# Five transposes per quad instead of six, norm sums on GpSimd, and a reordered step in a two-layer recurrent kernel

## The chip, the cores and the metric

The kernel runs on one core of a Trainium2 chip. The metric is device time in microseconds for one execution of the whole program. Engines are called by their profile names: PE (TensorE) for matmuls and transposes, DVE (VectorE), ACT (ScalarE), POOL (GpSimd), and SP (SyncE), whose queue issues the weight DMAs.

## The reference

Four residual layers are applied to x of 2048 rows by 640: memory attention A, local attention B, then A and B again with the same weights.

```python
def A(x, mem):                       # 32 heads of 192; 64 segments of 32 rows, one after another
    for s in range(64):
        h = concat([mem, x[32*s:32*s+32]])          # 8 memory rows + 32 rows
        q, k, v = h@Wq, h@Wk, h@Wv                  # 640 -> 32 heads x 192
        p = softmax(where(mask, q@k.T * 192**-0.5, -1e9))
        o = (p @ v) @ Wo
        mem = o[:8];  out.append(o[8:])             # the next segment needs this memory
def B(x):                            # 32 heads of 20; each row sees rows s, s-2, ..., s-14
    q, k, v = split(x @ wqkv)
    return (softmax over the 8 rows of q.k * 20**-0.5) @ v @ wo
x = x + A(layernorm(x)); x = x + B(layernorm(x))
x = x + A(layernorm(x)); x = x + B(layernorm(x))
```

## The kernel before

The two passes through A and B are run side by side as two lanes. In step t, lane 0 does segment t of the first A layer and lane 1 does segment t-2 of the second; the B layers of step t-1 run in the same step. There are 67 steps: two with lane 0 alone, 62 with both lanes, two with lane 1 alone, and a last one with only the B layer of the last segment, whose order is the short list LAST. A full step handles 80 columns in layer A (two lanes of 8 memory and 32 data rows) and 64 in layer B. Activations are kept transposed, features on the partitions.

The 32 heads of A are handled as eight quads. A quad has 768 features, six chunks of 128: heads of 192 features share a chunk in pairs, and chunks 1 and 4 are the shared ones. Per quad and step:

- K, Q, V: 30 matmuls each of 128x128 weights against 80 columns (L303). KE and VE copy the result to SBUF on ACT (L329, L342), QE on DVE.
- S: scores (L368). E: exponential on ACT (L374). EM: mask on DVE (L380).
- T: PE transposes V, chunk by chunk (L349), and TE copies the transposed chunks on DVE into Vt (L357, L358).
- PO: probabilities times V and the row sums (L401), from Vt. R: one over the row sums on ACT (L388 twice, L390). OT1, OT2: the product on DVE (L408, L413, L414).
- Oa, Ob: the two halves of the output matmuls (L420), which add into two PSUM buffers held for the whole step. Quad 7's are O7x, O7y, O7z.

V and its transpose before the change:

```python
vt = self.VT[:, 0:6 * NT].rearrange("p (a n) -> p a n", a=6)
self.nc.scalar.copy(out=vt[:, :, self.cs], in_=...six chunks of 80 columns...)
for n in range(6):
    nc.tensor.transpose(out=ps[:, n, :], in_=self.VT[:, NT * n:NT * n + P], identity=self.ident[:])
```

At the end of a step MEMa and MEMb (L454) cast the new memory rows into hT, the input of the next step's projections, and X1 (L510) adds the residual. The layer norm of the next A input is LSQ (squares and sums over chunks, L460 to L466), lst (a ones matmul that sums over partitions, L473), LMV (mean and variance on DVE), LR (two ACT operations, L490 and L492) and LAP (L500, L502). The B layer's norm is bsq, bst, bmv, br, bap with the same functions; then bq, bk, bv are the projections with bqE, bkE, bvE behind them, bs0 and bs1 the scores of each lane, be and eb their exponentials and masks, bt and btE the transpose of the values, bp, on, bo, boE, by, byE the rest. Both sums over chunks, of x and of its square, are DVE reductions:

```python
for j, v in enumerate((x, sq)):
    nc.vector.tensor_reduce(out=s[:, j, :], in_=v[:].rearrange("p c n -> p n c"), op=ALU.add, axis=mybir.AxisListType.X)
```

The order of everything is the hand-written list ORDER. Every engine executes its own instructions of the list strictly in that order, and waits where data or a buffer is missing. PSUM has four general buffers that are given out in turn to the K, Q, V, T, S, statistics and B results (the function `big`), one pair of banks for PO and two for the output sums. POOL has one instruction in a step, a copy that takes the next segment's rows (L655), at the head of the step.

The A weights are 128 pieces of 224 or 256 KB. N_RES = 79 of them stay in SBUF after their first load; the others are streamed in every step through a ring of eight buffers by SP's queue (L279), which waits until PE is done with the buffer. `resident_pieces` spreads the streamed ones evenly over the step by the positions in ORDER.

Of the kernel before, what the change touches and what calls it, by code (L numbers as in the profile page):

```python
# [38 lines left out]
N_RES = 79  # L39
PIECE = (8, 7)  # L40
O_ROWS = ((0, 2, 3), (5, 1, 4))

# [5 lines left out]
K0 Q0 bsq K0y QE0 KE0 V0 bst bmv VE0 Q1 S0 K1 T0 QE1 br bap E0 TE0 KE1 V1 S1 EM0 Q3 PO0 VE1 QE3 E1 bq T1 R0 K2  # L48
KE2 bqE TE1 Q2 K3 V2 QE2 OT10 S2 KE3 bk EM1 OT20 S3 PO1 VE2 E2 bkE Q4 T2 EM2 bs1 E3 QE4 V3 R1 K4 TE2 be1 VE3
Q5 OT11 OT21 KE4 PO2 R2 EM3 T3 eb1 bs0 be0 V4 QE5 Oa0 VE4 bv TE3 OT12 OT22 bvE Q6 S4 PO3 eb0 E4 bt R3 QE6 btE  # L50
K5 T4 EM4 K6 KE5 TE4 bp0 V5 OT13 Ob0 OT23 KE6 on0 S5 bp1 VE5 PO4 T5 Oa1 E5 R4 on1 TE5 V6 bo Q7 EM5 OT14 S6 boE
OT24 VE6 Ob1 E6 QE7 PO5 T6 EM6 TE6 by byE R5 K7 KE7 V7 S7 VE7 OT15 E7 OT25 LSQ PO6 EM7 Oa2 R6 T7 Ob2 Oa3 TE7
Ob3 OT16 OT26 Oa5 PO7 Oa6 R7 lst LMV Ob5 Oa4 Ob6 OT17 LR OT27 Ob4 LAP O7x O7y MEMa O7z MEMb X1
# [4 lines left out]
bsq bst bmv br bap bq bqE bk bkE bs0 be0 bv bs1 be1 eb0 bvE bt eb1 btE bp0 on0 bp1 on1 bo boE by byE  # L58
""".split()

def half_order():

    order = []
    for n in ORDER:
        if n[0] in "KQV" and len(n) == 2:
            order += [(n[0].lower(), int(n[1]), 0), (n[0].lower(), int(n[1]), 1)]
        elif n[:2] in ("Oa", "Ob"):
            order.append(("o", int(n[2]), int(n[1] == "b")))
        elif n == "O7x":
            order += [("o", 7, 0), ("o", 7, 1)]  # L70
    assert len(set(order)) == len(order) == 8 * NQUAD
    return order

def half_blocks(kind, i, h):

    if kind == "o":
        if i == NQUAD - 1:
            blocks = [(m, c) for c in range(NC) for m in O_ROWS[0] + O_ROWS[1]]
        else:
            blocks = [(m, c) for rows in O_ROWS for m in rows for c in range(NC)]  # L80
    elif (kind, i) == ("k", 0):
# [8 lines left out]
def resident_pieces():  # L90

    at, t = {}, 0.0
    for n in ORDER:
# [21 lines left out]
class Kernel:  # L115
    def __init__(self, ctx, tc, xT, m0T, wA, wqkv, wo, out):
# [22 lines left out]
        self.n_big = 0  # L139
        self.xt, self.ots, self.qxs, self.kp, self.qp, self.vp, self.tp = {}, {}, {}, {}, {}, {}, {}  # L140
# [3 lines left out]
    def build_consts(self):  # L144
# [33 lines left out]
        self.VT = pers("VT", [P, 6 * NT + 48], 1)[0]  # L178
# [112 lines left out]
    def span_of(self, t):  # L291
# [3 lines left out]
        self.cs = slice(LT * self.l0, LT * self.l1)  # L295

    def proj(self, ps, kind, i, h, t, chained=False):
# [3 lines left out]
        for k, (c, n) in enumerate(half_blocks(kind, i, h)):  # L301
            yield k
            self.nc.tensor.matmul(ps[:, NT * n + c0:NT * n + c1], lhsT=self.block(kind, i, h, k), rhs=hT[:, NT * c + c0:NT * c + c1],  # L303
# [36 lines left out]
    def vE(self, i):  # L340
        vt = self.VT[:, 0:6 * NT].rearrange("p (a n) -> p a n", a=6)
        self.nc.scalar.copy(out=vt[:, :, self.cs], in_=self.vp[i][:, 0:6 * NT].rearrange("p (a n) -> p a n", a=6)[:, :, self.cs])  # L342

    def a_t(self, i):

        nc = self.nc
        ps = self.big("ps_vt", (P, 6, P), BF16)
        for n in range(6):
            nc.tensor.transpose(out=ps[:, n, :], in_=self.VT[:, NT * n:NT * n + P], identity=self.ident[:])  # L349
        self.tp[i] = ps  # L350

    def tE(self, i):

        nc = self.nc
        ps, vt = self.tp[i], self.Vt[0:NT].rearrange("p (a j e) -> p a j e", a=2, e=P)
        src = ps[0:NT].rearrange("p (a j) e -> p a j e", a=2)
        nc.vector.tensor_copy(out=vt[:, :, 0:4:3, :], in_=src[:, :, 0:3:2, :])  # L357
        nc.vector.tensor_copy(out=vt[:, :, 1:3, 0:64], in_=src[:, :, 1, :].rearrange("p a (j e) -> p a j e", j=2))  # L358
# [75 lines left out]

    def acc_lanes(self, g):
# [20 lines left out]
    def ln_sq(self, x):  # L456
# [3 lines left out]
        nc.vector.tensor_tensor(out=sq[:], in0=x[:], in1=x[:], op=ALU.mult)  # L460
        s = self.bp.tile([P, 2, NX], F32, name="ln_s", tag="xc")
        for j, v in enumerate((x, sq)):
            nc.vector.tensor_reduce(out=s[:, j, :], in_=v[:].rearrange("p c n -> p n c"), op=ALU.add, axis=mybir.AxisListType.X)
        hl = sq[:].rearrange("p c n -> p (c n)")[:, 0:4 * NX].rearrange("p (j a n) -> p j a n", j=2, a=2)
        nc.vector.tensor_copy(out=hl[:, 0], in_=s[:])
        nc.vector.tensor_tensor(out=hl[:, 1], in0=s[:], in1=hl[:, 0], op=ALU.subtract)  # L466
        return hl

    def ln_stats(self, hl):
        nc = self.nc  # L470
        ps = self.big("ps_st")
        for j in range(2):
            nc.tensor.matmul(ps[:, 0:2 * NX], lhsT=self.ones[:], rhs=hl[:, j].rearrange("p a n -> p (a n)"), start=(j == 0), stop=(j == 1))  # L473
        return ps

    def ln_mv(self, ps):

        nc = self.nc
        m = self.bp.tile([P, NX], F32, name="ln_m")
        nc.vector.tensor_scalar(out=m[:], in0=ps[:, 0:NX], scalar1=1.0 / D, scalar2=None, op0=ALU.mult)  # L480
        v = self.bp.tile([P, NX], F32, name="ln_v")
        nc.vector.tensor_tensor(out=v[:], in0=m[:], in1=m[:], op=ALU.mult)
        nc.vector.scalar_tensor_tensor(out=v[:], in0=ps[:, NX:2 * NX], scalar=1.0 / D, in1=v[:], op0=ALU.mult, op1=ALU.subtract)
        return m, v

    def ln_r(self, mv):
# [366 lines left out]
```

The softmax here doesn't subtract the row's maximum and nothing guards it: scores larger than these inputs give would overflow.

## Time and profile before

| | |
|---|---|
| median of 3 runs | 3138.72 us (3137.41 to 3142.72) |
| profiled execution | 3140.52 us, span 3138.8 us |
| a step with both lanes | 46.6 us |
| last step, B layer alone | some 21 us |
| granted PE clock | 0.983 |

Three more lines of the page: the granted clock and the DMA share in 40 slices of the span, and the weight stream's issues. The clock is at full speed after the first 100 us and until the tail. The DMA engines are busy for eight tenths or more throughout, and a streamed piece lands 3.9 to 4.0 us after its issue.

```profile
PEclk6899999999999999999999999999999999999998
DMA  9988888888888888888888888888888888888885
...
w_ring<-in_wA_dram SPq DMA_DIRECT2D x1716, 256.0 KB, 3.9
```

### The profile page before, as it was taken

How to read it: one execution, taken by the hardware profiler on the slowest of the kernel's cores; microseconds unless marked ns; L12 is line 12 of the kernel's file. 1: busy time of each engine (PE TensorE's matmuls, PEld its weight loads, DVE VectorE, ACT ScalarE, POOL GpSimd, SP SyncE). 2: the span in 40 equal slices, each digit the busy share in tenths (PEclk: the TensorE clock that was granted, in tenths of full speed). 3: DMA queues.
4: the chain of work that ended last, by engine and by line, in shares of the span. 5: the costliest groups of instructions: out<-in, count | busy, mean ns of one | idle time of the engine just before them, and what ended most of it. 6: DMA issues, size and time to landing. Idle time of an engine off the chain costs nothing.

```text
span 3138.8 us, 185804 instructions
## 1 busy us (share of the span) xinstructions
PE 3063.2 (98%) x83160; PEld 3036.4 (97%) x83160; DVE 2358.2 (75%) x6883; ACT 1747.2 (56%) x3829; POOL 48.2 (2%) x162
## 2 busy tenths in 40 slices
PE   6899999999999999999999999999999999999996
PEld 5799999999999999999999999999999999999996
DVE  3577777777777777777777777777777777777775
ACT  2355556555556556556555655555655655655653
POOL 2000000000000000000000000000000000000000
PEclk6899999999999999999999999999999999999998
DMA  9988888888888888888888888888888888888885
GB/s 360 320 263 267 263 262 265 264 264 265 266 268 263 268 266 263 268 266 263 268 266 261 267 263 267 261 265 268 263 267 266 264 267 267 263 269 266 262 274 184
DMA packets 487807, 838.02 MB, mean 267 GB/s; under 512 B 54240, under 2 KB 261984, under 8 KB 487008
## 3 DMA queue, kind: packets, MB, share of 16 engines
q1 hardware_dynamic: 477648, 820.89, 83.2%
q8 instruction: 651, 10.67, 1.4%
q10 hardware_dynamic: 9360, 5.26, 0.6%
q14 instruction: 148, 1.21, 0.1%
HBM read 823.31 MB, written 2.62 MB: 263 GB/s over the span
## 4 chain that ended last, share of the span: by engine, by line
PE 95%; DMA 3%; issue 1%; DVE 1%; ACT 0%; SPq 0%; DVEq 0%; ACTq 0%
PE ps_k L303 18%; PE ps_q L303 18%; PE ps_v L303 18%; PE ps_vt L349 6%; PE ps_o L401 5%; PE ps_s L368 5%; PE ps_by L634 2%; PE ps_bq L523 2%; PE ps_bv L548 2%; PE ps_bk L523 2%; DMA w_ring<-in_wA_dram 1%; PE ps_bs L575 1%; PE ps_bo L598 1%; PE ps_bvt L561 1%; PE ps_st L473 0%
## 5 line engine op out<-in xcount | busy, mean ns | idle before, releaser
L303 PEld LDWEIGHTS <-w_ring 128*128 128x128 bf16 x17754 | 784.4, 100 | 19.4 <-DMA w_ring<-in_wA_dram 10.5
L388 ACT ACTIVATE R<-ps_o 64x320 f32<-64x320 f32 (+1 forms) x1056 | 448.5, 425 | 273.8 <-PE ps_o L401 223.6
L342 ACT CAST VT_140<-ps_v 128x480 bf16<-128x480 f32 (+1 forms) x528 | 288.9, 547 | 230.7 <-PE ps_v L303 227.6
L329 ACT CAST KF_121<-ps_k 128x480 bf16<-128x480 f32 (+1 forms) x264 | 144.1, 546 | 391.2 <-PE ps_k L303 383.3
L374 ACT ACTIVATE Em<-ps_s 80x320 bf16<-80x320 f32 (+1 forms) x528 | 223.3, 423 | 157.2 <-PE ps_s L368 110.7
L420 PEld LDWEIGHTS <-w_ring 128*128 128x128 bf16 x6600 | 291.2, 100 | 3.5 <-DMA w_ring<-in_wA_dram 2.6
L335 DVE CAST QT_127<-ps_q 128x320 bf16<-128x320 f32 (+1 forms) x264 | 127.1, 481 | 203.4 <-PE ps_q L303 203.4
L357 DVE COPY Vt_134<-ps_vt 80x512 bf16<-80x512 bf16 x528 | 219.2, 415 | 71.5 <-PE ps_vt L349 69.3
L349 PE MATMUL ps_vt<-ident,VT_140 128*128 128x128 bf16 x3168 | 267.7, 221 | 0.0
L408 DVE TENSOR_TENSOR OT<-ps_o,R 128x320 bf16<-128x320 f32 (+1 forms) x528 | 249.9, 473 | 22.3 <-ACT R L390 16.6
L329 ACT CAST KF_123<-ps_k 128x480 bf16<-128x480 f32 (+1 forms) x264 | 144.1, 546 | 205.6 <-PE ps_k L303 203.9
L390 ACT ACTIVATE R<-R 128x320 f32<-128x320 f32 (+1 forms) x528 | 244.0, 462 | 16.6
L401 PE MATMUL ps_o<-Em,Vt_134 80*128 80x80 bf16 (+1 forms) x4224 | 238.0, 199 | 1.4 <-issue 1.3
L335 DVE CAST QT_125<-ps_q 128x320 bf16<-128x320 f32 (+1 forms) x264 | 126.5, 479 | 143.1 <-PE ps_q L303 71.9
L349 PEld LDWEIGHTS <-VT_140 128*128 128x128 bf16 x3168 | 191.5, 99 | 0.1
L303 PE MATMUL ps_q<-hT_92,w_ring 128*128 128x80 bf16 (+1 forms) x3234 | 185.8, 201 | 3.7 <-DMA w_ring<-in_wA_dram 2.6
L303 PE MATMUL ps_q<-hT_90,w_ring 128*128 128x80 bf16 (+1 forms) x3234 | 186.3, 201 | 2.2 <-DMA w_ring<-in_wA_dram 1.5
L401 PEld LDWEIGHTS <-Vt_134 80*128 80x128 bf16 x4224 | 181.6, 98 | 1.0 <-issue 0.7
L303 PE MATMUL ps_k<-hT_90,w_ring 128*128 128x80 bf16 (+1 forms) x3003 | 172.7, 201 | 1.4 <-DMA w_ring<-in_wA_dram 0.7
L303 PE MATMUL ps_k<-hT_92,w_ring 128*128 128x80 bf16 (+1 forms) x3003 | 171.8, 201 | 1.4 <-issue 1.4
L380 DVE TENSOR_TENSOR Em<-Em,maskA 80x320 bf16<-80x320 bf16 (+1 forms) x528 | 163.2, 309 | 12.5 <-ACT Em L374 8.4
L414 DVE TENSOR_TENSOR OT<-ps_o,R 64x160 bf16<-64x160 f32 (+1 forms) x528 | 165.1, 313 | 7.3
(3084 smaller groups left out, 8305.2 us busy)
## 6 DMA issues: line engine op xcount, KB each, us to landing
w_ring<-in_wA_dram SPq DMA_DIRECT2D x1716, 256.0 KB, 3.9
w_ring<-in_wA_dram SPq DMA_DIRECT2D x1518, 224.0 KB, 4.0
out_dram<-YT_94 ACTq DMA_DIRECT2D x32, 80.0 KB, 3.7
wqkv_sb<-in_wqkv_dram SPq DMA_DIRECT2D x3, 800.0 KB, 7.7
wo_sb<-in_wo_dram SPq DMA_DIRECT2D x1, 800.0 KB, 7.4
w_k_00_386<-in_wA_dram SPq DMA_DIRECT2D x1, 256.0 KB, 2.8
w_k_10_405<-in_wA_dram SPq DMA_DIRECT2D x1, 256.0 KB, 3.8
w_q_10_438<-in_wA_dram SPq DMA_DIRECT2D x1, 256.0 KB, 4.6
```

Of the source, the lines that this page charges most:

```text
L303: self.nc.tensor.matmul(ps[:, NT * n + c0:NT * n + c1], lhsT=self.block(kind, i, h, k), rhs=hT[:, NT * c + c0:NT * c + c1], start=(h == 0 ...
L329: self.nc.scalar.copy(out=kf[:, :, self.cs], in_=self.kp[i][:, 0:6 * NT].rearrange("p (a n) -> p a n", a=6)[:, :, self.cs])
L335: nc.vector.tensor_copy(out=qt[:, :, 0:4:3, cs], in_=pv[:, :, 0:3:2, cs])
L342: self.nc.scalar.copy(out=vt[:, :, self.cs], in_=self.vp[i][:, 0:6 * NT].rearrange("p (a n) -> p a n", a=6)[:, :, self.cs])
L349: nc.tensor.transpose(out=ps[:, n, :], in_=self.VT[:, NT * n:NT * n + P], identity=self.ident[:])
L357: nc.vector.tensor_copy(out=vt[:, :, 0:4:3, :], in_=src[:, :, 0:3:2, :])
L374: self.nc.scalar.activation(out=e[0:NT, :, cs], in_=self.sv[i][0:NT, :, cs], func=ACT.Exp, scale=float(DH) ** -0.5)
L388: self.nc.scalar.activation(out=r[rows, :, :, self.cs], in_=d, func=ACT.Ln)
L390: self.nc.scalar.activation(out=rf, in_=rf, func=ACT.Exp, scale=-1.0)
L401: nc.tensor.matmul(ov[:, pr, b, self.cs], lhsT=vt[0:NT, 512 * pr + P * b:512 * pr + P * (b + 1)], rhs=em[0:NT, 2 * pr + b // 2, self.cs], ...
L408: self.nc.vector.tensor_tensor(out=ot[:, :, 0:3:2, cs], in0=self.ov[:, :, 0:4:3, cs], in1=self.r[i][:, :, :, cs], op=ALU.mult)
L420: self.nc.tensor.matmul(self.acc[c // 3][:, o:o + self.cs.stop - self.cs.start], lhsT=self.block("o", i, h, k), rhs=ot[:, m, self.cs], sta ...
```

## The change

Four things are changed, and ORDER with them.

1. The V result's chunk 1 is put first in PSUM (V_AT). VE copies the other five chunks as before, and puts chunk 1, cut into column groups of 32, 32 and 16, into columns 96 to 127 of the first three. Five transposes then carry all six chunks: rows 0 to 79 of the result hold five chunks, rows 96 to 127 the three pieces of chunk 1. TE copies the five on DVE, and the new step TF copies the three pieces on ACT.
2. The sum over chunks of x, in both layer norms, becomes three additions on POOL. The sum of squares stays on DVE.
3. The second output half of quad 6 is sorted by output chunk and runs as O6x and O6y; the statistics of the next A norm (lst, LMV) stand before PO7.
4. In the last step the B layer's norm, masks and expansions handle only lane 1's 32 columns, and bs0, be0, eb0 are left out of LAST.

VT grows, and N_RES falls from 79 to 78.

```diff
-N_RES = 79
+N_RES = 78
+V_AT = (1, 0, 2, 3, 5, 4)
...
 ORDER = """
-K0 Q0 bsq K0y QE0 KE0 V0 bst bmv VE0 Q1 S0 K1 T0 QE1 br bap E0 TE0 KE1 V1 S1 EM0 Q3 PO0 VE1 QE3 E1 bq T1 R0 K2
...
-OT24 VE6 Ob1 E6 QE7 PO5 T6 EM6 TE6 by byE R5 K7 KE7 V7 S7 VE7 OT15 E7 OT25 LSQ PO6 EM7 Oa2 R6 T7 Ob2 Oa3 TE7
-Ob3 OT16 OT26 Oa5 PO7 Oa6 R7 lst LMV Ob5 Oa4 Ob6 OT17 LR OT27 Ob4 LAP O7x O7y MEMa O7z MEMb X1
+K0 bsq K0y KE0 Q0 V0 QE0 bst Q1 S0 bmv VE0 QE1 E0 T0 br K1 TE0 KE1 TF0 V1 Q2 VE1 EM0 S1 PO0 bap QE2 E1 V2 R0
...
+bp1 OT22 QE5 E4 PO3 on1 EM4 R3 V5 T4 VE5 TE4 K6 OT13 Q6 S5 TF4 OT23 bp0 PO4 KE6 Oa0 Ob0 E5 QE6 on0 T5 R4 S6
+TE5 EM5 OT14 E6 V6 TF5 OT24 Q7 QE7 VE6 bo Ob1 PO5 boE T6 by TE6 R5 K7 TF6 byE EM6 KE7 OT15 V7 OT25 VE7 S7 PO6
+Oa2 E7 LSQ T7 Ob2 R6 Oa3 EM7 lst TE7 OT16 Ob3 Oa4 TF7 OT26 LMV PO7 Oa6 Oa5 O6x R7 OT17 OT27 Ob4 Ob5 O6y LR LAP
+O7x O7y MEMa O7z MEMb X1
 LAST = """
-bsq bst bmv br bap bq bqE bk bkE bs0 be0 bv bs1 be1 eb0 bvE bt eb1 btE bp0 on0 bp1 on1 bo boE by byE
+bsq bst bmv br bap bk bkE bq bqE bv bs1 be1 bvE eb1 bt btE bp0 on0 bp1 on1 bo boE by byE
...
     def vE(self, i):
-        vt = self.VT[:, 0:6 * NT].rearrange("p (a n) -> p a n", a=6)
-        self.nc.scalar.copy(out=vt[:, :, self.cs], in_=self.vp[i][:, 0:6 * NT].rearrange("p (a n) -> p a n", a=6)[:, :, self.cs])
+        ps, cs, copy = self.vp[i], self.cs, self.nc.scalar.copy
+        copy(out=self.VT[:, :, cs], in_=ps[:, NT:6 * NT].rearrange("p (a n) -> p a n", a=NC)[:, :, cs])
+        if cs.stop - cs.start == NT:
+            copy(out=self.VT[:, 0:3, P - 32:P], in_=ps[:, 0:96].rearrange("p (a n) -> p a n", a=3))
...
     def a_t(self, i):
-        for n in range(6):
-            nc.tensor.transpose(out=ps[:, n, :], in_=self.VT[:, NT * n:NT * n + P], identity=self.ident[:])
+        for n in range(NC):
+            nc.tensor.transpose(out=ps[:, n, :], in_=self.VT[:, n, :], identity=self.ident[:])
...
+    def tF(self, i):
+        ps = self.tp[i]
+        two = lambda v: v.rearrange("p (j e) -> p j e", j=2)[:, :, 0:64]
+        for j in range(3):
+            n = min(NT - 32 * j, 32)
+            self.nc.scalar.copy(out=two(self.Vt[32 * j:32 * j + n, 128:384]), in_=ps[96:96 + n, j, :].rearrange("p (j e) -> p j e", j=2))
...
     def ln_sq(self, x):
-        nc.vector.tensor_tensor(out=sq[:], in0=x[:], in1=x[:], op=ALU.mult)
-        for j, v in enumerate((x, sq)):
-            nc.vector.tensor_reduce(out=s[:, j, :], in_=v[:].rearrange("p c n -> p n c"), op=ALU.add, axis=mybir.AxisListType.X)
+        add(s[:, 2:4, ns], x[:, 0:2, ns], x[:, 2:4, ns])
+        add(s[:, 2, ns], s[:, 2, ns], s[:, 3, ns])
+        add(s[:, 0, ns], s[:, 2, ns], x[:, 4, ns])
+        nc.vector.tensor_tensor(out=sq[:, :, ns], in0=x[:, :, ns], in1=x[:, :, ns], op=ALU.mult)
+        nc.vector.tensor_reduce(out=s[:, 1, ns], in_=sq[:, :, ns].rearrange("p c n -> p n c"), op=ALU.add, axis=mybir.AxisListType.X)
```

Here `add` is a `nc.gpsimd.tensor_tensor` and `ns` the rows in use (`b_rows`), all 64 except in the last step.

## The prediction

> **What bounds the kernel now.** I read the page's busy table first, then the list of TensorE's waits, then one step of the timeline.
>
> ```profile
> PE 3063.2 (98%) x83160; PEld 3036.4 (97%) x83160; DVE 2358.2 (75%) x6883; ACT 1747.2 (56%) x3829; POOL 48.2 (2%) x162
> ...
> L349 PE MATMUL ps_vt<-ident,VT_140 128*128 128x128 bf16 x3168 | 267.7, 221 | 0.0
> ```
>
> TensorE is busy nearly always, and its matmuls overlap, so the 221 ns of a transpose are latency, not its share of the time. The chain of waits lists six transposes as one piece of 0.34 us, 0.056 us each. From 160 to 3028 us the waits view gives TensorE under 5 us of waiting in all. But its matmul ends are modelled, so a gap shorter than the drain doesn't show there. The timeline of the end of a step shows one (columns: start, length, engine and line, operation, count):
>
> ```profile
> 1533.25 0.46 PE L401 MATMUL ps_o<-Em,Vt_134 80*128 80x80 bf16 x8
> ...
> 1537.17 0.42 PE L420 MATMUL ps_acc_51496<-OT,w_o_11_1962 128*128 128x80 bf16 x7
> 1537.61 0.45 PE L303 MATMUL ps_k<-hT_90,w_k_00_386 128*128 128x80 bf16 x8
> ```
> ```profile
> 1533.80 0.88 ACT L388 ACTIVATE R<-ps_o 64x320 f32<-64x320 f32 x2 [1.68 <-PE ps_o L401]
> 1534.71 0.47 ACT L390 ACTIVATE R<-R 128x320 f32<-128x320 f32 x1
> ```
> ```profile
> 1535.21 0.49 DVE L408 TENSOR_TENSOR OT<-ps_o,R 128x320 bf16<-128x320 f32 x1
> ...
> 1536.29 0.49 DVE L500 TENSOR_TENSOR ln_xc<-xin_86,ln_m 128x320 f32<-128x320 bf16 x1
> 1536.88 0.56 DVE L502 TENSOR_TENSOR hT_90<-ln_xc,ln_r 128x160 bf16<-128x160 f32 x2
> 1537.36 0.20 DVE L454 CAST hT_90<-ps_acc_51495 128x48 bf16<-128x48 f32 x1
> ```
>
> Projection matmuls start 0.0358 us apart (30 in 1.075). Seven from 1537.17 are issued by 1537.42, yet K0 of the next step starts at 1537.61: 0.19 us idle, in each of the steps that I looked at. What ends that gap is the memory cast at 1537.56, and behind it a chain without a hole: PO7, R7, OT17 and OT27, LAP, MEMa. So a step has two parts. From K0 to PO7 (1491.18 to 1533.25, 42.07 us) TensorE's own work decides. From PO7 to the next K0 (4.36 us) a ScalarE and VectorE chain decides, and TensorE work put there only fills it.
>
> **What the Trainium skill says.** "TensorE: Matmul & The Clock Gate", section "Back-to-back issue gap", gives N/2.4 + 2.5 ns for a warm matmul, 55.8 ns at 128 columns; the trace's 0.34/6 agrees. "ScalarE: Activation LUTs", section "What ACT_TABLE_LOAD costs", gives 186 ns + 0.833 ns per element and an overlap of 93 ns between neighbours. The trace is a little cheaper (480 elements 546 ns, 320 elements 425). "GPSIMD Engine Reference", section 3.1, gives a two-input add about 2.6 cycles an element at 1.2 GHz, 2.2 ns; the trace has such an add only at 10 elements, at 203 ns.
>
> **The change part by part.** A full step is one with both lanes, from the K0 at 138.04 to that at 3028.21: 62 of them, 46.62 us each.
>
> Transposes: eight quads lose one each, 8 x 0.0558 = 0.446 us of TensorE work per step, all before PO7.
>
> The first layer's statistics matmul (lst, 0.11 us) moves from behind PO7 to before it. Output halves: nine before PO7 and five behind it, in both orders. So the first part becomes 42.07 - 0.446 + 0.111 = 41.74 us. The second part is the same chain in the same order on ScalarE and VectorE, so 4.36 us; TensorE's work there falls by 0.11, and the gap before K0 grows from 0.19 to 0.30. Step: 46.10 against 46.43, **-0.335 us**, over 62 steps **-20.8 us**.
>
> ScalarE: the V copy of 480 elements (0.547) becomes 400 (0.486, between the rows at 320 and 480) and 96 (0.25, from the row of 240 at 0.36), and three copies of 128 elements (0.275 each by the same slope) are new: +1.0 us a quad, 8 us a step, from 57% to about 75% busy. I cost it at nothing, and T7 is the place to test that: 2.27 us of TensorE work (four output halves and lst) lie between T7 and PO7, the least of the eight. After PO6 ScalarE runs R6 (1.38) and TF7 (about 0.65, neighbours overlapping), ready 2.3 us after PO6; PO7 comes 3.09 us after it. Behind TF7 on ScalarE stands only R7, which waits for PO7 anyway. For T4, the next (2.6 us), the PSUM buffer is wanted again by bp0, behind TF4 in the order. If a TF came too late the PV matmuls and the whole TensorE queue would wait; bounds 0 to 0.4 us a step, I take 0.03.
>
> VectorE: the second transpose copy falls from 256 to 128 elements (0.277 to 0.21) and a 0.70 us reduction leaves each of two norms: some 2 us a step less, hidden behind TensorE and so worth nothing, except in the tail.
>
> GpSimd: three dependent adds per norm. This is the added wait that I fear. X1 ends 0.67 us after K0 starts; GpSimd's queue then has the copy of the next rows (0.41), done at 1.21. Only then come the adds, of 128, 64 and 64 elements. Estimate: 203 ns at 10 elements plus 2.2 ns for each further one gives 0.46, 0.32, 0.32, and 0.1 between them (the idle time in the row of the small adds): 1.3 us, done at 2.6. The VectorE cast and subtraction (0.26 and 0.29) wait for them, done at 3.2; behind them in VectorE's queue stand QE0, then bmv. TensorE reaches the second bst matmul at 0.86 + 0.215 + 1.075 + 1.075 + 0.056 = 3.28 us. So there is hardly any margin: every tenth above 1.4 us for the three adds stops TensorE by a tenth per step. Bounds: 1.0 us if an add costs like GpSimd's one-input operations (nothing lost), 1.8 if sharing with VectorE slows them (0.4 lost). I take 0.03 us a step. The same adds for LSQ run while VectorE still has byE, EM6 and OT15 ahead, and hide.
>
> One resident piece fewer: 50 streamed pieces a step for 49, 0.92 us apart for 0.95. SyncE's queue waits for ring buffers that TensorE frees; eight buffers give about 7.4 us against 3.9 to 4.0 to landing, so it hides: 0, bounds 0 to +2 us in all. I count +0.3 for the first steps, where the weights are still arriving and TensorE waits for them. Output chunks O6 in two parts: same matmuls and weights, inside the second part of the step, nothing. The single-lane steps at both ends keep their gaps: -0.5 together.
>
> Tail. After the last output chunk the local layer runs alone for some 21 us, a chain from X1 to the store. With one lane: one reduction and the sums (1.55 us of VectorE) become three small adds (about 0.95) and the cast and subtraction shrink, -0.75; the three LN operations, the two of ScalarE and the single h2T multiply -0.4; the key product goes first and QX halves, but the value product now stands before bs1, +0.2; two exponentials instead of four (this row is 2.41 us) -1.2.
>
> ```profile
> 3118.55 0.68 DVE L463 TENSOR_REDUCE ln_s<-x_369 128x64 f32<-128x320 bf16 x1
> ...
> 3124.36 1.49 DVE L539 TENSOR_TENSOR QX<-ps_bq,pair_mask 128x1280 bf16<-128x1280 f32 x1 [1.58 <-PE ps_bq L523]
> ```
> ```profile
> 3126.79 2.41 ACT L581 ACTIVATE EB_142<-ps_bs 64x512 bf16<-64x512 f32 x4 [4.61 <-PE ps_bs L575]
> ```
>
> Tail together -2.2 us (bounds -3.5 and 0).
>
> Sum: -20.8 + 62 x 0.06 (3.7 for the two waits) - 2.2 - 0.5 + 0.3 = -19.5. Against the profiled span of 3138.8 that is 3119.3. That execution took 3140.5 by the clock of the other runs, whose median is 3138.7, so spans stand level with the median within 0.1%. I forecast 3119 us.
>
> **The rivals.** *The chain does not bind.* If the 4.36 us shrink with the work (say the gap before K0 has another cause, such as the step's own first weights), the whole 0.446 us counts: -27.7 - 2.2 - 0.5, 3108.5 us. For it: the waits view names no such wait. Against: MEMa ends 0.05 us before K0 starts.
>
> *GpSimd's adds become the bound,* at bst, early in each step. Price: each step loses what the three adds take above 1.4 us. At 1.77 us the per-step gain is gone; at 2.0 us a step is 0.6 - 0.335 = 0.265 us longer, 16 us in all, less the tail: 3153 us, slower than before. It decides from about 1.9 us. For it: the margin is zero by my sum, and no row shows such adds at size. Against: the estimate is 1.3 us, and VectorE, from which a disturbance would come, has only a one-input reduction to do then.
>
> *ScalarE comes late,* 0.05 us on each of eight quads: 0.4 a step eats the gain, 3141 us. For it: 8 us more a step in a strict queue. Against: 0.8 us of margin at the tightest place.
>
> **How the numbers follow.** The forecast's case (3112 to 3125) has 0.57, the chain not binding 0.15, adds or ScalarE taking a part (3125 to 3132) 0.11, taking all of it 0.08, and slower than before 0.09, most of it GpSimd. About 0.2%, 6.3 us, is what a measurement here can tell from no change: faster 0.83, same 0.08, slower 0.09. The range runs from 3107 to 3133 us.
>
> **What would show it.** Right: five transposes in 0.28 us; the K0 gap near 0.3 us; steps of about 46.3 us on average; a tail near 19 us; QX and the exponentials halved there. Wrong: VectorE's cast waiting long for GpSimd and TensorE idle before bst; ScalarE's copies of L387 ending just before PO; the K0 gap unchanged at 0.19 or less.

## The result, and the profile after

The changed kernel takes 3121.67 us (median of 3 runs, 3118.93 to 3122.74), 0.9941 of the time before, with a 95% interval of 0.9918 to 0.9964. The forecast was 3119 us, with a range of 3107 to 3133. The profiled execution took 3118.93 us, with a span of 3117.2 us against 3138.8.

First the busy table of the page after, the group of the transposes and that of the new copies (busy us, mean ns of one, idle time before).

```profile
PE 3036.5 (97%) x82627; PEld 3009.9 (97%) x82627; DVE 2257.5 (72%) x6748; ACT 2204.5 (71%) x5971; POOL 199.7 (6%) x558
...
L387 ACT COPY Vt_136<-ps_vt 32x128 bf16<-32x128 bf16 (+1 forms) x1584 | 411.2, 260 | 32.2 <-DVE Vt_136 L379 6.1
...
L369 PE MATMUL ps_vt<-ident,VT_142 128*128 128x128 bf16 x2640 | 237.4, 221 | 1.2 <-ACT Em L403 0.9
```

The transposes fall from 3168 to 2640. ScalarE goes from 56% to 71% busy, most of it the 411 us of the TF copies. VectorE falls from 75% to 72%, and GpSimd is at 6%. TensorE keeps its 97%: the work has gone, and the time with it.

The timeline of the same end of a step as before (start, length, engine and line, operation, count):

```profile
1524.33 0.46 PE L430 MATMUL ps_o<-Em,Vt_136 80*128 80x80 bf16 x8
...
1528.14 0.42 PE L449 MATMUL ps_acc_52529<-OT,w_o_11_1998 128*128 128x80 bf16 x7
1528.70 0.45 PE L315 MATMUL ps_k<-hT_90,w_k_00_388 128*128 128x80 bf16 x8
```
```profile
1524.88 0.88 ACT L417 ACTIVATE R<-ps_o 64x320 f32<-64x320 f32 x2 [0.85 <-PE ps_o L430]
...
1526.29 0.49 DVE L437 TENSOR_TENSOR OT<-ps_o,R 128x320 bf16<-128x320 f32 x1 [1.24 <-ACT R L419]
...
1528.44 0.20 DVE L488 CAST hT_90<-ps_acc_52528 128x48 bf16<-128x48 f32 x1
```

From PO7 at 1524.33 to the next K0 at 1528.70 are 4.37 us, as before. The seven matmuls that start at 1528.14 are issued by 1528.39, so TensorE is idle for 0.31 us ahead of K0, where it was idle for 0.19. The memory cast still ends just before K0 starts (1528.64). That is the prediction's picture.

For the rest I take lengths from the start times of the matmuls in the two traces, since their ends are modelled. "Full steps" are the 62 with both lanes. Their median matters more than their mean: a few stops ("issue", no wait that the profile shows), tied to no place, add 11 to 12 us to the full steps of either kernel (counted from the shortest step), between 2 and 20 us in the runs below, and 82 in the last of them. Where such stops fall in every second step, the median holds some of them too, and the shortest step is given beside it.

| part of the span (us) | before | after | difference | predicted |
|---|---|---|---|---|
| full steps, all 62 | 2890.2 | 2870.8 | -19.4 | -17.1 (-20.8 and 3.7 for waits) |
| one full step, median | 46.439 | 46.117 | -0.322 | -0.335 |
| start to the first full step | 138.0 | 139.2 | +1.2 | +0.3 |
| single-lane steps at the end | 89.4 | 87.4 | -2.0 | -0.5 |
| tail, from the last X1 | 21.15 | 19.8 | -1.4 | -2.2 |
| sum of the four | 3138.8 | 3117.2 | -21.6 | -19.5 |

The first part and the single-lane steps differ by 1 to 4 us between runs that have the same code there, so nothing can be read from their rows. The medians of the executions are 17.1 us apart and not 21.6: the execution profiled after the change was the fastest of its three, the one before was 1.8 us above its median.

The new adds at bsq, in the same step, timeline of GpSimd, VectorE and TensorE:

```profile
1482.92 0.47 POOL L703 COPY xin_86<-XT_50115 128x160 bf16<-128x160 bf16 x1 [8.79 <-DVE x_371 L552]
1483.35 0.42 POOL L496 TENSOR_TENSOR ln_s<-x_371 128x128 f32<-128x128 bf16 x1
...
1484.25 0.31 POOL L496 TENSOR_TENSOR ln_s<-ln_s,x_371 128x64 f32<-128x64 f32 x1
```
```profile
1484.59 0.23 DVE L503 CAST sq<-ln_s 128x128 bf16<-128x128 f32 x1 [0.62 <-POOL ln_s L496]
1484.86 0.29 DVE L504 TENSOR_TENSOR sq<-ln_s,sq 128x128 bf16<-128x128 f32 x1
...
1485.50 0.28 PE L511 MATMUL ps_st<-sq,ones 128*128 128x128 bf16 x2
```

The three adds, the one left out here of 0.32 us, take 1.21 us (estimated: 1.3). VectorE stands still for 0.62 us until they end, in every step, and TensorE doesn't notice: the subtraction ends at 1485.15, and the second bst matmul starts 0.4 us later, in its turn.

In the tail, TensorE, VectorE and ScalarE:

```profile
3104.11 1.52 PE L596 MATMUL ps_bv<-h2T_373,wqkv_sb 128*128 128x64 bf16 x25
3104.34 0.83 DVE L583 TENSOR_TENSOR QX<-ps_bq,pair_mask 128x640 bf16<-128x640 f32 x1 [0.84 <-PE ps_bq L565]
3105.45 0.72 PE L623 MATMUL ps_bs<-QX,KX_375 128*128 128x128 bf16 x5
3106.21 1.19 ACT L629 ACTIVATE EB_144<-ps_bs 64x512 bf16<-64x512 f32 x2 [5.14 <-PE ps_bs L623]
```

QX and the exponentials are halved (0.83 for 1.49 us, 1.19 for 2.41). But bs1 starts at 3105.45, 0.28 us after QX ends: the 25 matmuls of bv stand ahead of it.

### The profile page after: what moved, and what is told of

It reads as the page before. It is cut to its first block, busy times and chain, and to the rows that moved or that the text cites. A ratio compares the mean times of both kernels' runs of the same rounds, so it can differ in the third digit from the quotient of the medians.

```text
span 3117.2 us, 187910 instructions
## 1 busy us (share of the span) xinstructions
PE 3036.5 (97%) x82627; PEld 3009.9 (97%) x82627; DVE 2257.5 (72%) x6748; ACT 2204.5 (71%) x5971; POOL 199.7 (6%) x558
## 3 DMA queue, kind: packets, MB, share of 16 engines
HBM read 836.09 MB, written 2.62 MB: 269 GB/s over the span
## 4 chain that ended last, share of the span: by engine, by line
PE 87%; DVE 5%; ACT 3%; DMA 3%; issue 1%; SPq 0%; ACTq 0%; POOL 0%; DVEq 0%; POOLq 0%
PE ps_k L315 18%; PE ps_v L315 18%; PE ps_q L315 18%; PE ps_o L430 5%; PE ps_vt L369 5%; PE ps_s L397 5%; ACT R L417 2%; PE ps_bk L565 2%; PE ps_bq L565 2%; PE ps_by L682 2%; PE ps_bv L596 2%; DMA w_ring<-in_wA_dram 1%; PE ps_bs L623 1%; DVE ln_xc L542 1%; DVE OT L437 1%
## 5 line engine op out<-in xcount | busy, mean ns | idle before, releaser
L315 PEld LDWEIGHTS <-w_ring 128*128 128x128 bf16 x18348 | 811.3, 100 | 13.6 <-DMA w_ring<-in_wA_dram 10.6
L387 ACT COPY Vt_136<-ps_vt 32x128 bf16<-32x128 bf16 (+1 forms) x1584 | 411.2, 260 | 32.2 <-DVE Vt_136 L379 6.1
L355 ACT CAST VT_142<-ps_v 128x400 bf16<-128x400 f32 (+1 forms) x528 | 254.7, 482 | 154.5 <-PE ps_v L315 138.7
L449 PEld LDWEIGHTS <-w_ring 128*128 128x128 bf16 x6402 | 282.1, 100 | 7.5 <-issue 3.9
L369 PE MATMUL ps_vt<-ident,VT_142 128*128 128x128 bf16 x2640 | 237.4, 221 | 1.2 <-ACT Em L403 0.9
L315 PE MATMUL ps_k<-hT_90,w_ring 128*128 128x80 bf16 (+1 forms) x3531 | 202.3, 201 | 3.1 <-DMA w_ring<-in_wA_dram 2.2
L315 PE MATMUL ps_q<-hT_90,w_ring 128*128 128x80 bf16 (+1 forms) x3432 | 198.7, 201 | 2.3 <-DMA w_ring<-in_wA_dram 1.6
L315 PE MATMUL ps_k<-hT_92,w_ring 128*128 128x80 bf16 (+1 forms) x3531 | 200.8, 201 | 0.1
L315 PE MATMUL ps_q<-hT_92,w_ring 128*128 128x80 bf16 (+1 forms) x3432 | 197.9, 201 | 2.4 <-DMA w_ring<-in_wA_dram 2.0
```

Of the source, the lines that this page charges most:

```text
L355: copy(out=self.VT[:, :, cs], in_=ps[:, NT:6 * NT].rearrange("p (a n) -> p a n", a=NC)[:, :, cs])
L369: nc.tensor.transpose(out=ps[:, n, :], in_=self.VT[:, n, :], identity=self.ident[:])
L387: self.nc.scalar.copy(out=two(self.Vt[32 * j:32 * j + n, 128:384]), in_=ps[96:96 + n, j, :].rearrange("p (j e) -> p j e", j=2))
L449: self.nc.tensor.matmul(self.acc[c // 3][:, o:o + self.cs.stop - self.cs.start], lhsT=self.block("o", i, h, k), rhs=ot[:, m, self.cs], sta ...
```

## The experiments

Two theories stand at the beginning. Mine, A, is the prediction's: from K0 to PO7 TensorE's own work decides, so a transpose fewer counts whole, and lst, moved ahead of PO7, costs its 0.11 us; behind PO7 a chain of fixed length decides. The rival, B, is that another chain already decides in front of PO7. The reason for B is in the trace. The last piece of OT26, before and after:

```profile
1532.88 0.32 DVE L414 TENSOR_TENSOR OT<-ps_o,R 64x160 bf16<-64x160 f32 x1
```
```profile
1523.96 0.32 DVE L443 TENSOR_TENSOR OT<-ps_o,R 64x160 bf16<-64x160 f32 x1
```

Before the change it ends at 1533.20 and PO7 starts at 1533.25; after it, at 1524.28 and 1524.33. Ratios are to the kernel before on the same chip, with 95% intervals; where none is given there was one execution. On the chips used the kernel before took 3133.6 to 3140.5 us, so the times of two experiments can't be set side by side. "Step" is the median of the 62 full steps.

**Six transposes in the new order.** The old vE, a_t and tE with their buffer; no TF; all else as changed.

```diff
-V_AT = (1, 0, 2, 3, 5, 4)
+V_AT = (0, 1, 2, 3, 4, 5)
...
-K0 bsq K0y KE0 Q0 V0 QE0 bst Q1 S0 bmv VE0 QE1 E0 T0 br K1 TE0 KE1 TF0 V1 Q2 VE1 EM0 S1 PO0 bap QE2 E1 V2 R0
+K0 bsq K0y KE0 Q0 V0 QE0 bst Q1 S0 bmv VE0 QE1 E0 T0 br K1 TE0 KE1 V1 Q2 VE1 EM0 S1 PO0 bap QE2 E1 V2 R0
```

> The changed kernel with six transposes per quad again: the old V copy of 480 columns, six transposes, the old two VectorE copies and no ScalarE copies; everything else as changed. Theory A (five transposes are where the time comes from): each step regains 8 x 0.056 = 0.45 us of TensorE work, less what of the last transpose falls into a wait, so a full step goes from 46.12 to 46.5 to 46.57 us and the time from about 3121 to 3145 to 3149, above the kernel before. Rival (the ScalarE copies cost as much as the transposes give, and the gain is from the new order): the step stays at 46.1, the time at 3121.

Measured: 3134.1 us, ratio 1.0001 (0.9993 to 1.0009), step 46.503. In the new order the transposes with their copies are the whole gain, 0.386 us a step. Without them the new order, the moved lst and GpSimd's sums together cost 0.064 us a step. Eight transposes are 0.446, so 0.06 is lost; the section on the prediction says where.

**Both sums on VectorE.**

```diff
-        add(s[:, 2:4, ns], x[:, 0:2, ns], x[:, 2:4, ns])
-        add(s[:, 2, ns], s[:, 2, ns], s[:, 3, ns])
-        add(s[:, 0, ns], s[:, 2, ns], x[:, 4, ns])
+        nc.vector.tensor_reduce(out=s[:, 0, ns], in_=x[:, :, ns].rearrange("p c n -> p n c"), op=ALU.add, axis=mybir.AxisListType.X)
```

> The changed kernel with both sums over chunks on VectorE again. Theory A (the sums lie beside TensorE work in every full step): full steps unchanged at 46.11 to 46.13 us, bst not waited for, the tail about 0.4 us longer, the time the same within 1 us. Rival (VectorE is short of time at the step's ends, so taking 1.4 us a step off it is part of the gain): steps longer by 0.1 us or more, the time longer by 6 us or more.

Measured: 3111.43 us, ratio 0.9928 (0.9915 to 0.9942), step 46.116. The step is the same to 0.001 us, so GpSimd's sums are worth nothing there. The tail is 19.0 us against 19.8 in the changed kernel, where I had expected it to be longer. Part of that is spread: the changed kernel's own tail was 19.5 us in another run. But the stretch from X1 to the first projection is 0.15 us shorter than with the adds in both of them (3.92 against 4.07 and 4.09). So what the changed kernel gains there comes from the halved columns, not from GpSimd.

**lst and LMV back behind PO7.**

```diff
-Oa2 E7 LSQ T7 Ob2 R6 Oa3 EM7 lst TE7 OT16 Ob3 Oa4 TF7 OT26 LMV PO7 Oa6 Oa5 O6x R7 OT17 OT27 Ob4 Ob5 O6y LR LAP
+Oa2 E7 LSQ T7 Ob2 R6 Oa3 EM7 TE7 OT16 Ob3 Oa4 TF7 OT26 PO7 Oa6 lst LMV Oa5 O6x R7 OT17 OT27 Ob4 Ob5 O6y LR LAP
```

> The changed kernel with lst and LMV behind PO7 again, as before the change. Theory A (TensorE's own work decides when PO7 starts, so lst ahead of it costs 0.11 us a step): step 46.12 - 0.11 = 46.01 us, gap before K0 down from 0.30 to 0.19, time shorter by about 6.9 us. Theory B (PO7 waits for OT26 already: the chain begins at V7, through VE7, E7, R6, OT16 and OT26): PO7 does not come earlier, an idle gap of about 0.15 us opens before PO7 while the one before K0 falls to 0.19, and the step stays at 46.1 us, the time the same within 2 us.

Measured: 3110.66 us, ratio 0.9927 (0.9914 to 0.9939), step 46.117, as with lst in front. The time of lst has moved from one idle gap to another: TensorE's gap before K0 goes from 0.30 to 0.19 us, the one before PO7 from 0.05 to 0.165. PO7 still starts 0.05 us after OT26 ends:

```profile
1519.71 0.32 DVE L443 TENSOR_TENSOR OT<-ps_o,R 64x160 bf16<-64x160 f32 x1
...
1520.08 0.46 PE L430 MATMUL ps_o<-Em,Vt 80*128 80x80 bf16 x8
```

B is right. PO7 waits for OT26, which frees its PSUM pair, and lst in front of it costs nothing. The step of A that charged 0.111 us for lst falls.

**One output half more behind PO7.** If a gap of 0.30 us stands before K0, work from in front of PO7 should fill it. Oa4 goes behind PO7 and Ob1 into its place; quad 5's OT gets a buffer of its own, since Ob1 now reads quad 1's after OT15.

```diff
-TE5 EM5 OT14 E6 V6 TF5 OT24 Q7 QE7 VE6 bo Ob1 PO5 boE T6 by TE6 R5 K7 TF6 byE EM6 KE7 OT15 V7 OT25 VE7 S7 PO6
-Oa2 E7 LSQ T7 Ob2 R6 Oa3 EM7 lst TE7 OT16 Ob3 Oa4 TF7 OT26 LMV PO7 Oa6 Oa5 O6x R7 OT17 OT27 Ob4 Ob5 O6y LR LAP
+TE5 EM5 OT14 E6 V6 TF5 OT24 Q7 QE7 VE6 bo PO5 boE T6 by TE6 R5 K7 TF6 byE EM6 KE7 OT15 V7 OT25 VE7 S7 PO6
+Oa2 E7 LSQ T7 Ob2 R6 Oa3 EM7 lst TE7 OT16 Ob3 Ob1 TF7 OT26 LMV PO7 Oa6 Oa5 Oa4 O6x R7 OT17 OT27 Ob4 Ob5 O6y LR LAP
...
-        ot = self.ap1.tile([P, 2, 3, NT], BF16, name="OT", tag=f"OT{i % 4}")
+        ot = self.ap1.tile([P, 2, 3, NT], BF16, name="OT", tag=f"OT{4 if i == 5 else i % 4}")
```

> The changed kernel with two output halves moved later: Oa4 from before PO7 to behind it, Ob1 from before PO5 into Oa4's place between PO6 and PO7; quad 5's attention output gets a buffer of its own so that Ob1 may come so late. The same work in all. Theory B (from V7 to the next K0 a ScalarE and VectorE chain of about 7.9 us sets the pace and TensorE has only about 7.7 us to do there): 0.54 us more work behind PO7 fills the gap before K0, which vanishes; the step falls by about 0.30 to 45.8 us, the time by 18 us to about 3103. Rival (the gap before K0 comes with the first weights of the step or the engine's own start, whatever stands before it): the gap stays at 0.3 us and the step at 46.1. Second rival (Ob1 later holds up PO5 or PO6): the gap moves to another place in the step, time unchanged or longer.

Measured: 3115.44 us, ratio 0.9942 (0.9929 to 0.9956), step 45.954, that is 0.163 less (0.30 was expected) and the shortest of all. The gap before K0 is gone: the last output matmul and K0 start 0.071 us apart, where it was 0.339. But 0.13 us of a new gap stands before by in each step:

```profile
1510.52 0.43 ACT L674 CAST OTB<-ps_bt 128x320 bf16<-128x320 f32 x1 [0.41 <-PE ps_bt L669]
...
1510.99 0.89 PE L682 MATMUL ps_by<-OTB,wo_sb 128*128 128x64 bf16 x25
```

With Ob1 gone from between bo and by, TensorE reaches by before ScalarE's copy of OTB ends (1510.95). In time the version is not to be told from the changed kernel.

**The same with bo earlier.** To give boE time, bo and boE go ahead.

```diff
-TE5 EM5 OT14 E6 V6 TF5 OT24 Q7 QE7 VE6 bo PO5 boE T6 by TE6 R5 K7 TF6 byE EM6 KE7 OT15 V7 OT25 VE7 S7 PO6
+TE5 EM5 OT14 E6 V6 TF5 OT24 bo Q7 QE7 boE VE6 PO5 T6 by TE6 R5 K7 TF6 byE EM6 KE7 OT15 V7 OT25 VE7 S7 PO6
```

> The kernel with the two output halves moved later, and in addition bo ahead of Q7 and boE ahead of VE6, so that by no longer follows bo by only PO5 and T6. Theory B (chain from V7 to K0, filled by the moved halves; what was left was 0.13 us of waiting before by in every step): by is not waited for, the step falls from 45.95 to 45.83 us, 0.29 us below the changed kernel, 18 us in all: ratio to before about 0.989 to 0.990. Rival (the chain has slid along with the work and a gap opens elsewhere, before PO5, PO6 or PO7): the step stays at 45.95.

Measured: 3124.42 us, ratio 0.996 (0.9947 to 0.9974), step 46.279; the shortest is 46.104, and 25 of the 62 are within 0.01 us of it. The 0.13 us before by are gone, but a gap of 0.26 us stands before Q7 in every step. PSUM buffers go round in turn, and bo ahead of Q7 gives Q7 the buffer of T5, which TF5 must have emptied. So the undisturbed step is 0.15 us longer than with bo in its old place and as long as in the changed kernel. The rival in the expectation is right that a gap opens elsewhere, though at a place that it didn't name.

**The same with by later instead.** by and byE stand behind K7, from the version with one half behind.

```diff
-TE5 EM5 OT14 E6 V6 TF5 OT24 Q7 QE7 VE6 bo PO5 boE T6 by TE6 R5 K7 TF6 byE EM6 KE7 OT15 V7 OT25 VE7 S7 PO6
+TE5 EM5 OT14 E6 V6 TF5 OT24 Q7 QE7 VE6 bo PO5 boE T6 TE6 R5 K7 by TF6 EM6 byE KE7 OT15 V7 OT25 VE7 S7 PO6
```

> The kernel with two output halves moved later (its step was 45.95 us, with 0.13 us of waiting before by), and now by behind K7 instead of in front of R5 and K7, EM6 ahead of byE on VectorE. bo stays where it was, since moving it made Q7 wait for quad 5's PSUM buffer. Theory: OTB is ready long before by, the buffers come free in time, and the step falls to 45.82 to 45.85 us, 0.28 us below the changed kernel, some 17 us in all, although the time of one run also depends on rare stops of TensorE of 4 to 14 us in all that are not tied to a place. Rival: the work moved behind byE (the norm of the next rows) comes late for lst or LMV and a gap opens there: 45.95 or more.

Measured: 3135.45 us, ratio 0.9983 (0.9974 to 0.9992), step 46.363 (the shortest 46.242, with 22 of the 62 within 0.01 us of it). I had missed VectorE's queue:

```profile
1523.08 0.32 DVE L692 TENSOR_TENSOR xin<-ps_by,x 128x160 bf16<-128x160 f32 x1 [0.97 <-PE ps_by L682]
...
1524.27 0.32 DVE L443 TENSOR_TENSOR OT<-ps_o,R 64x160 bf16<-64x160 f32 x1
```

byE now waits 0.97 us for by, and OT15 and OT25 stand behind it. OT25 ends at 1524.59, and PO6, which needs its PSUM pair, starts at 1524.64, 0.35 us late.

**The changed kernel again.**

> The changed kernel itself once more, beside the kernels of the same call on the same chip. Both theories: full steps of 46.12 us, gap before K0 0.30 us, 0.993 to 0.995 of the time before.

Measured: 3123.13 us, ratio 0.9955 (0.9942 to 0.9967), step 46.118, gap before K0 as before.

**The transposes alone.** The kernel before with the five transposes, its old order, and TF right behind TE (quad 7's one later).

```diff
-Q5 OT11 OT21 KE4 PO2 R2 EM3 T3 eb1 bs0 be0 V4 QE5 Oa0 VE4 bv TE3 OT12 OT22 bvE Q6 S4 PO3 eb0 E4 bt R3 QE6 btE
+Q5 OT11 OT21 KE4 PO2 R2 EM3 T3 eb1 bs0 be0 V4 QE5 Oa0 VE4 bv TE3 TF3 OT12 OT22 bvE Q6 S4 PO3 eb0 E4 bt R3 QE6 btE
```

> The kernel before, in its old order, with the five transposes alone: the new V copies, TF right behind TE in the order (one step later for quad 7), 78 resident pieces; sums on VectorE and the last step as before. If the transposes are the whole gain of a full step: 0.39 us (seven transposes before PO6, and the eighth lost to the wait of PO7 for OT26) to 0.45 us off 46.44, that is 46.0 to 46.05 us, as short as the changed kernel's 46.12 or shorter. Rival (the ScalarE copies need the new order to be hidden): steps above 46.15 us, with TensorE waiting for ScalarE's copies at PO or T.

Measured: 3415.07 us, ratio 1.0885 (1.087 to 1.09), step 50.94: 4.5 us longer than before, where TensorE has 0.446 less to do. From its list of waits (waiting engine and releaser; us in total, times, longest):

```profile
ACT Vt L378 <- DVE Vt L370: 320.0, 268, 3.6
...
PE ps_s L388 <- ACT KF L332: 121.6, 127, 1.5
```

ScalarE stands at TF until VectorE has made its two copies of TE. What is behind TF on ScalarE comes late, above all the copies of K, and TensorE waits for those at S, and at Q6 for the PSUM buffer of T3, which TF3 must have emptied (93.1 us in 63 times). From start to start of its matmuls, TensorE stops in a step for 1.64 us before Q6, 1.42 before S1, 0.82 before S7, 0.58 before PO7, 0.30 before T3 and 0.20 before PO6 (medians). That is 4.96 us; less the 0.446 saved it makes the 4.5.

**TF behind TE in the new order.** How much of that is the place of TF, how much the rest of the order? The changed kernel, with each TF directly behind its TE.

```diff
-TE5 EM5 OT14 E6 V6 TF5 OT24 Q7 QE7 VE6 bo Ob1 PO5 boE T6 by TE6 R5 K7 TF6 byE EM6 KE7 OT15 V7 OT25 VE7 S7 PO6
+TE5 TF5 EM5 OT14 E6 V6 OT24 Q7 QE7 VE6 bo Ob1 PO5 boE T6 by TE6 TF6 R5 K7 byE EM6 KE7 OT15 V7 OT25 VE7 S7 PO6
```

> The changed kernel with every TF directly behind its TE in the order; nothing else differs. It tells whether the 4.5 us a step that the five transposes cost in the old order came of the old order or of where TF stood in ScalarE's queue. If of TF's place (ScalarE stops at TF until VectorE has reached TE, and every copy and exponential behind it is late): well above 46.12 us, 47.5 or more. If of the old order: up to 46.5.

Measured: 3179.8 us, step 47.135, 1.02 more than changed and between the two values expected. Its list of waits names the same engines:

```profile
ACT Vt L387 <- DVE Vt L379: 140.5, 143, 5.1
...
PE ps_s L397 <- ACT KF L341: 41.6, 64, 0.9
```

TensorE's new gaps in a step are one of 0.82 us before S7 and one of 0.20 before PO6. So the place of TF is worth 1.0 us a step in the new order. The same two gaps, of the same length, stand in the version with the transposes alone; its four others, at Q6, S1, PO7 and T3, 3.9 us together, are there in the old order only.

**Two more adds in each norm.** They write a row of ln_s that nothing reads any more, so that GpSimd's chain is longer and the result the same.

```diff
+        for _ in range(2):
+            add(s[:, 3, ns], s[:, 2, ns], x[:, 4, ns])
         add(s[:, 0, ns], s[:, 2, ns], x[:, 4, ns])
```

> The changed kernel with two more dependent additions of 64 elements on GpSimd in every norm, whose results nothing uses. It tests the place where GpSimd's adds would become the bound. By the changed kernel's trace the statistics are ready 0.35 to 0.4 us before the second bst matmul, and two more adds take about 0.78 us: TensorE then stands idle before bst for 0.35 to 0.45 us and the step grows from 46.12 to 46.5 us. As the prediction had it (no loss up to 1.4 us for the adds, here about 2.0): 0.6 us, a step of 46.7. Rival (a stall at bst is made good later in the step): 46.12.

Measured: 3132.83 us, step 46.383 (46.331 the shortest), 0.21 to 0.27 more than changed. In the step whose K0 starts at 1440.86:

```profile
1442.81 0.95 POOL L496 TENSOR_TENSOR ln_s<-ln_s,x 128x64 f32<-128x64 f32 x3
...
1443.79 0.23 DVE L505 CAST sq<-ln_s 128x128 bf16<-128x128 f32 x1 [1.27 <-POOL ln_s L496]
...
1444.08 0.53 PE L513 MATMUL ps_st<-sq,ones 128*128 128x128 bf16 x2
```

The adds end at 1443.76, 2.90 us after K0 starts, and TensorE then loses 0.26 to 0.28 us between the two bst matmuls (drawn as 0.53 for two, where it was 0.28). So the limit is 2.62 to 2.64 us after K0. In the changed kernel the adds end some 2.27 us after K0, 0.35 to 0.4 us inside it.

**bv behind bs1 in the last step.**

```diff
-bsq bst bmv br bap bk bkE bq bqE bv bs1 be1 bvE eb1 bt btE bp0 on0 bp1 on1 bo boE by byE
+bsq bst bmv br bap bk bkE bq bqE bs1 be1 bv bvE eb1 bt btE bp0 on0 bp1 on1 bo boE by byE
```

> The changed kernel with bv behind bs1 and be1 in the short order of the last step. In the changed kernel bs1 starts 0.28 us after QX is ready, when bv's 25 matmuls at the lower clock are issued. Theory: bs1 starts 0.25 us earlier and the tail, from X1 to the end of the program, falls from 19.8 to about 19.5 us, full steps unchanged. Rival (bv then comes late for bvE): the tail unchanged or longer.

Measured: 3124.98 us. bs1 starts 0.06 us after QX ends instead of 0.28, and 7.83 us after X1 instead of 8.05. The whole tail is 19.68 us, between the two runs of the changed kernel (19.8 and 19.49), so a gain of that size at the end can't be told.

**Six resident pieces fewer.**

```diff
-N_RES = 78
+N_RES = 72
```

> The changed kernel with 72 resident pieces instead of 78: 56 pieces streamed in a step for 50, one every 0.82 us. Theory (the stream is hidden behind TensorE): full steps stay at 46.12 us, DMA share up from 0.87 to about 0.95, and the two single-lane steps at the end, which need about 0.65 us a piece, stay within 1 us. Rival (the stream is near its limit, so that the one piece given up already costs): steps longer by 0.1 us or more, with TensorE waiting for the ring.

Measured: 3194.36 us; mean step 47.44 against 46.30, that is 70 us over 62 steps. For the middle of each run, 200 to 3000 us, the changed kernel and then this one (busy us of PE, PEld, DVE, ACT, POOL; then PE clock, DMA share, GB/s):

```profile
200.00:3000.00 2800.00, 2786.10 (x75732) 2775.49 (x75729) 2090.66 (x6168) 2048.79 (x5449) 162.70 (x419) 1.00 0.87 271
```
```profile
200.00:3000.00 2800.00, 2744.89 (x73957) 2718.59 (x73953) 2043.67 (x6022) 1998.16 (x5317) 160.16 (x413) 1.00 0.91 295
```

And of the waits of the second, 160 to 3000 us:

```profile
PEld L315 <- issue: 45.2, 113, 2.0
```

The waits for the ring itself are 10 us (9.8, in 16 times). Most of TensorE's stops bear no wait at all ("issue", 45 us; 19 in the changed kernel over the same stretch). Part of both is the gap before K0, which this view books as "issue" too: 12 of the 45 and 15 of the 19. Elsewhere it is 34 us against 4. Between the stops a step is as short as ever, 46.113 us.

My reading is that these stops are late instructions, which come by DMA as well (the page lists a queue "q8 instruction"; its packets are of 16 KB, one every 4.8 us). The packets of the trace speak for it. Of the 82 places in this stretch where two TensorE matmuls start more than 0.4 us apart, 74 go on between 1.15 and 1.70 us after such a packet has landed; a moment taken at random lies so in 11% of cases. In the changed kernel it is 9 of 12 and in the kernel before 8 of 9. That ties the stops to these packets in time. No run here changed how the instructions come, so the cause isn't shown. The rival in the expectation is right that the stream isn't free, though not in that TensorE waits for the ring.

## Why the prediction was right, and where it wasn't

**The transposes.** Right: 0.056 us each, five in 0.28. Seven of the eight lie in front of PO6, where TensorE's own work decides, and bring 7 x 0.0558 = 0.39 us: K0 to PO6 goes from 38.728 to 38.333.

**From PO6 to PO7.** This is the step that failed. The prediction counted TensorE's work there: a transpose less and lst more, +0.055 us. In truth a chain decides: VE7, E7, R6, OT16, OT26, PO7. That its length grew by about as much, +0.07, and the step came out as forecast, is luck. The chain was in the trace before: PO7 starts 0.057 us after OT26 ends (median of the full steps), in both kernels. Before the change TensorE would have been ready only 0.04 us sooner, so there the two nearly tie. In the changed kernel the chain is longer for another reason. ScalarE's timeline, before and after:

```profile
1529.83 0.56 ACT L342 CAST VT_140<-ps_v 128x480 bf16<-128x480 f32 x1 [0.52 <-PE ps_v L303]
1530.28 0.43 ACT L374 ACTIVATE Em<-ps_s 80x320 bf16<-80x320 f32 x1
1530.74 0.88 ACT L388 ACTIVATE R<-ps_o 64x320 f32<-64x320 f32 x2
```
```profile
1520.83 0.49 ACT L355 CAST VT_142<-ps_v 128x400 bf16<-128x400 f32 x1 [0.32 <-PE ps_v L315]
1521.22 0.24 ACT L357 CAST VT_142<-ps_v 128x96 bf16<-128x96 f32 x1
1521.35 0.44 ACT L403 ACTIVATE Em<-ps_s 80x320 bf16<-80x320 f32 x1
1521.82 0.88 ACT L417 ACTIVATE R<-ps_o 64x320 f32<-64x320 f32 x2
```

VE7, now in two copies, starts at the same place against PO6 (0.08 us ahead of it) but delays E7: 0.52 us from one to the other for 0.455. R6 stands behind E7, and from R6's start to the end of OT26 it is 2.458 us in both kernels. So PO6 to PO7 goes from 3.348 to 3.421 us: +0.07. With -0.39 that makes the -0.32 measured. The prediction's "+0.111 for lst" is 0, and its "nothing" for ScalarE's V copies is 0.07 us a step at this one quad. Two runs bear this out. With six transposes and the old VE7, E7 follows after 0.456 us and TensorE decides: PO7 starts 0.13 us after OT26, 3.423 us after PO6. (So there lst in front does cost something, and the 0.064 us that this version loses to the kernel before stand here, 3.423 against 3.348.) That is no more than with five transposes, so the one that T7 saves is the 0.06 us lost. With lst behind PO7, PO6 to PO7 is still 3.421. A VE7 in one piece beside five transposes was not tried. By these numbers TensorE's own work would then set 3.423 - 0.056 = 3.37 us, so an estimate of what the split costs is 0.05 us a step.

**From PO7 to K0.** Right: 4.362 us before, 4.363 after, a gap of 0.19 that becomes 0.30. The version with one output half more behind PO7 shows it from the other side: there TensorE's work fills the gap, and the stretch becomes 4.63 us. The rival that the chain doesn't bind is out.

**ScalarE.** TF was estimated at 0.65 us and takes 0.80: three copies of 0.26 us start 0.27 apart, without the overlap of about 93 ns that the Trainium skill, "ScalarE: Activation LUTs", section "What ACT_TABLE_LOAD costs", gives for back-to-back ACTIVATE instructions. At T7 the prediction saw TF7 ready 2.3 us after PO6, 0.8 us before PO7. It is ready 3.1 us after PO6 (at 1524.02), 0.3 us before PO7, mostly because R6, in front of TF7, starts only 0.9 us after PO6: E7 is still in its way on ScalarE. That ScalarE's 8 us more are hidden is true of this order alone: with TF at another place they cost 1.0 us a step, in the old order a net 4.5 us. The prediction's rival "ScalarE comes late", priced at 0.4 us a step, is what the transposes do without the rest of the change, at some ten times the price.

**GpSimd.** The term of the adds was nearly right, 1.21 us for 1.3, and the limit of 2.6 us after K0 is confirmed by the two more adds (2.62 to 2.64). The margin was put at nothing and is 0.35 to 0.4 us: the adds began earlier (1.07 us after K0's start for 1.21) and were shorter, and subtraction and cast are done 0.59 us after the adds, as expected. Part of it was a slip in the sum: 1.21 and 1.3 make 2.51, not 2.6, and with 0.55 for cast and subtraction 3.06, which left 0.2 us before 3.28. So the rival of GpSimd as the bound had its limit in time right and its price a little high (the adds may take some 1.56 us before TensorE stops, not 1.4); it is out by a third of a microsecond. The gain of moving the sums is nothing.

**The waits.** 3.7 us were put by for ScalarE and GpSimd coming late; the full steps show none of it.

**The stream.** "It hides: 0" was too sure. One piece fewer shows no cost in the step (46.117 is within 0.01 us of the shortest step, and TensorE's gaps are accounted for), but six more cost 1.1 us a step, with buffers and landing times that by my argument should have held. Waits for ring buffers were not the thing to look at; what grew were TensorE's stops without a recorded wait.

**The tail.** -1.4 us for -2.2. From X1 to the first projection -1.11 (predicted -1.15) is right. From there to the first scores it is +0.50 where I had +0.2, and from the scores to the last exponential -0.95 for -1.2. The exponentials themselves bring their 1.2 (2.41 to 1.19 us); most of what is missing at both places is TensorE's granted clock. It was 0.50 from 3101 us to the end of the changed kernel, and 1.00 from 3126.5 to 3128 us in the kernel before, where scores and bv run. So the 25 matmuls of bv held TensorE for 1.33 us, and the five of bs1 took 0.72 us for 0.45. In the version with two more adds, with the same order, the clock was 1.00 from 3118.7 us on, at bv; bv was through when QX ended, and bs1 started 0.06 us later:

```profile
3118.61 0.92 PE L598 MATMUL ps_bv<-h2T,wqkv_sb 128*128 128x64 bf16 x25
3118.84 0.82 DVE L585 TENSOR_TENSOR QX<-ps_bq,pair_mask 128x640 bf16<-128x640 f32 x1 [0.84 <-PE ps_bq L567]
3119.72 0.44 PE L625 MATMUL ps_bs<-QX,KX 128*128 128x128 bf16 x5 [0.18 <-DVE QX L585]
```

By the last exponential that had given back the 0.5 us that the longer adds cost in the tail. So bv's place costs 0.23 us at the lower clock and nothing at the higher. Why the clock was lower in one and not the other, no run here shows. The end, from YT to the last instruction, is 0.2 us longer, and varies by that much.

What stays open: the versions with VectorE sums and with lst behind PO7 have ratios near 0.9927, the changed kernel 0.9941 and 0.9955, at the same step to 0.001 us. The difference lies in the rare stops and the single-lane steps, and I found no cause for it. Those two ran on the same chip, the second run of the changed kernel on another.

## What to carry to other kernels

A matmul that starts a few hundredths of a microsecond after another engine's instruction ends may be waiting for it, even where no view lists a wait: look for such pairs before work in front of it is counted as time, test them by taking that work away, and follow the chain behind it on its strict queue, where splitting one copy in two is a cost. An edit that takes work from the busiest engine and gives more to a strict queue elsewhere is only as good as the place that it gets there: the same five transposes went with -0.32 us, +0.7 us or +4.5 us a step against the kernel before. Where a gap is left in front of a chain's end, moving work into it pays (-0.16 us a step here, too little to be seen in the time), but each move takes time from some other wait: of three versions that did so, two had nothing of it left.

## What the runs showed of the hardware

- The first GpSimd add, of 128 elements on 128 partitions, takes 0.425 us at bsq, where VectorE is reducing one input, and 0.60 us at LSQ (medians of 66 in the changed kernel), where VectorE is multiplying two inputs from SBUF (Em by its mask). Where one of VectorE's two inputs came from PSUM instead, in the version with by later, it took 0.43 us at LSQ as well. The Trainium skill, "GPSIMD Engine Reference", section "1. Specifications", says that GpSimd's SBUF interfaces are shared with VectorE and that there is contention with VectorE instructions of two SBUF inputs; the three numbers agree. The additions of 64 elements took 0.31 to 0.32 us. The slow one, in the changed kernel:

```profile
1519.15 0.60 POOL L496 TENSOR_TENSOR ln_s<-xin_86 128x128 f32<-128x128 bf16 x1 [34.59 <-DVE xin_86 L692]
1519.16 0.31 DVE L409 TENSOR_TENSOR Em<-Em,maskA 80x320 bf16<-80x320 bf16 x1
```

- TensorE's stops without a recorded wait grew with the weight stream: away from K0, from 4 to 34 us at PEld of L315 when the DMA share went from 0.87 to 0.91. With six resident pieces fewer, 74 of the 82 longer ones ended 1.15 to 1.70 us after a packet of the instruction queue had landed.
